# Where the block sums of y are split, and the order of ACT's bank copies, in an attention, mixture-of-experts and feed-forward kernel

## Chip, cores and metric

The kernel runs on one core of one Trainium2 chip. Times are microseconds (us) of device time for one execution; the time of a version is the median of its runs. The engines are TensorE (PE; its weight loads are listed apart as PEld), VectorE (DVE), ScalarE (ACT), GpSimd (Pool) and SyncE (SP), which issues nearly all DMAs, in order.

## What is computed

Three parts in a row on 2304 tokens of 512 values, all in float32.

```python
# 1. linear attention, 4 x 8 heads, 576 tokens, head size 64
kv = einsum('bhsd,bhse->bhde', k, v); out = einsum('bhsd,bhde->bhse', q, kv)
x = out / sqrt(mean(out * out) + 1e-6) * g_norm          # then to (2304, 512)
# 2. mixture of experts: 8 experts, 512 -> 1024 -> 512, one expert per token
expert_idx = argmax(x @ w_gate)
y = gate_w * (relu(x_e @ w1[e]) @ w2[e])                 # tokens beyond the capacity give 0
# 3. feed-forward: 512 -> 2048 -> 512
h = y @ w_in
out = where(h > 0, h, exp(min(h, 0)) - 1) @ w_out        # ELU
```

## The kernel before

Every float32 matrix product is made of three products of a faster type: a tile `t` is split into a high part `th` (an ACT copy that rounds, `split_hi`) and a low part `tl = t - th` (a subtraction on DVE or Pool, `split_lo`), and PE multiplies high by high, low by high and high by low (`three`, L636). So each operand that PE gets costs ACT one copy and DVE or Pool one subtraction.

**Expert steps.** The tokens are sorted by expert, and the experts run in order of falling load, each in NF = 8 steps, 64 in all (`step(u)`, L917). A step issues the weights of step u + 3 on SP (`expert_load`, two tiles of 256 KB), multiplies the tokens by 128 columns of w1 (`expert_h(u)`: 12 matmuls, then `hh` on ACT and `hl` on DVE from the bank `ph`), multiplies the hidden values of the step before by w2 (`expert_y(u - 1)`: 12 matmuls) and splits the weights of step u + 2 (`expert_split`). Some steps also convert a weight of the feed-forward part (`next(parts)`) or split the next expert's tokens (`window`). The order on every engine is the written one (`manual_schedule`). In the middle, after step 36, stands a branch that all engines take together.

**Block sums.** Three of the four quarters of the feed-forward part (by hidden columns) are computed in pairs of token blocks by Strassen's way (seven products instead of eight); its right operands are differences of blocks of y. The 2304 tokens are NB = 6 blocks of BT = 384, in three pairs m; for each pair and each of KH = 2 column groups k there are four differences, 24 in all. `right_sums` (L876) is a generator that makes one a call: it first finishes the one before (low part on DVE, then two DMAs of 192 KB on SP to `y_dram`), then subtracts on DVE into `tr`, and copies the high part into `th` on ACT. `th` and `tl` share the tag "e", two buffers for the two of them; `tr` has two buffers of tag "g". The first 16 sums (pairs 0 and 1) are called at the end of the expert steps listed in `SUMS` (37, 38, 40, 44, 45, 46, 48, 52, 53, 54, 56, 60, 61, 62, 63, 64) and the last finish in step 1 of the second layer; the eight of pair 2 (`late_sums`) in steps 1 to 9 of that layer, in spare halves of the output tile `part`.

**Second layer, first quarter.** `ffn_step(s)`, 24 steps (six blocks, four chunks of 128 hidden columns each): 12 matmuls of 384 columns, ELU (two ACT activations, `e`, and one DVE operation, `g`), its split `gh`, `gl` in the next step, and 9 matmuls of 512 columns two steps later into three accumulator banks of four; after a block's last chunk ACT copies the banks to `part` (L1029). In each block's second step the next block of y is split (`y_block_into`): four ACT copies, four Pool subtractions, DMAs. Two banks hold `ph`. One piece of weight preparation a step (`next(parts2)`) issues a load two pieces ahead.

**Second layer, the other quarters.** `pair_step(w, s)` (L1124), nine windows w of a pair and a quarter, two steps each. A step makes seven products of 6 matmuls, P1, P5, P2, P6, P3, P7, P4 in that order. P1, P6, P7, P4 accumulate on top of each other in the bank `pa`, P5 and P3 in `pd`, P2 in `pe`, and ACT copies the bank out between them (`s1`, `s5`, `u2`, `u3`), so that the next product into `pa` waits for the copy. Four blocks come out (c11, c12, c22, c21), each goes through `elu` and `elu_split`. In the gaps between products stand weight preparation (`gap`) and the units that multiply by w_out, whose sums DVE adds to `part`; at the end Pool scatters `part` to the output. The first six windows have the written order, the last three the order of the compiler's scheduler.

The lines that the change is about, of the sums:

```python
for ... in sums of a piece:            # right_sums, L890
    if last:
        finish()                       # split_lo (DVE) and 2 DMAs of the sum before
    r, t = tiles()
    nc.vector.tensor_tensor(out=r, in0=x, in1=y, op=ALU.subtract)
    split_hi(t, r)                     # ACT
    last.append((m, o, k, r, t))
    yield
```

Of the kernel before, what the change touches and what calls it, by code (L numbers as in the profile page):

```python
# [20 lines left out]
P = 128  # L21
# [20 lines left out]
def block_kernel(ctx, tc, qT, k, v, g_norm, w_gate, w1, w2, w_in, w_out, out, cap, **_):  # L42
# [13 lines left out]
    NB = 6  # L56
# [463 lines left out]
    def split_hi(dst, src):  # L520
        return nc.scalar.activation(dst[0], src, AF.Copy)  # L521

    def split_lo(dst, src, engine):
        return engine.tensor_tensor(out=dst[1], in0=src, in1=dst[0].bitcast(F32), op=ALU.subtract)  # L524
# [348 lines left out]
            for h, t in enumerate((yh, yl)):  # L873
                nc.sync.dma_start(out=y_dram[n // 2, o][:, h], in_=t[:, k:k + KH].bitcast(F32))

    def right_sums(pieces, tiles):  # L876


        last = []

        def finish():
            m, o, k, r, t = last.pop()
            split_lo(t, r, nc.vector)
            for h in range(2):
                nc.sync.dma_start(out=y_dram[m, o][:, h, k], in_=t[h].bitcast(F32))

        for m, k in pieces:
            b = [[yT[:, h * KH + k, (2 * m + n) * BT:(2 * m + n + 1) * BT] for n in range(2)] for h in range(2)]
            r = None
            for o, x, y in ((5, b[1][1], b[0][1]), (3, b[0][1], b[0][0]), (4, b[1][1], None), (6, b[1][0], None)):  # L890
                if last:
                    finish()
                y = r if y is None else y
                r, t = tiles()
                nc.vector.tensor_tensor(out=r, in0=x, in1=y, op=ALU.subtract)
                split_hi(t, r)
                last.append((m, o, k, r, t))
                yield
        finish()
        yield  # L900

    def small_tiles():
        t = [hp.tile([P, BT], F32R, name=n, tag="e", bufs=2) for n in ("th", "tl")]
        return hp.tile([P, BT], F32, name="tr", tag="g", bufs=2), t


    assert 3 * (N // E) >= 2 * BT and 6 * (N // E) >= 4 * BT
    early_sums = right_sums([(m, k) for m in range(2) for k in range(KH)], small_tiles)
    SUMS = [u for u in range(4 * NF + 5, NU) if u % NF in (0, 4, 5, 6)]
    SUMS = SUMS[:8] + [u for u in SUMS[8:] if u > 6 * NF] + [NU - 1, NU]  # L910

    APART = 4 * NF + 4
    FIRST = NF + 1
# [3 lines left out]
    def step(u):  # L917
        r, fc = divmod(u, NF)
        if u == 4:
            nc.gpsimd.memset(xT[:, :, N:NS], 0.0)  # L920
        more = r + 1 < E and placed["t"] < need[r + 1]
        expert_load(u + 3)
        if u == FIRST - 1:
            prep_load(2)
# [19 lines left out]
        if u == APART:  # L944
            place(NT, 0)
            beyond_windows()
        if u in SUMS:
            next(early_sums, None)
        if u == NU - 2 and cap >= BT:
            y_block_into(0)  # L950

# [79 lines left out]


    spare = part[:, NT // 2:].rearrange("p i c -> p (i c)")
    turn = {"n": 0}

    def spare_tiles():
        n = turn["n"] = 1 - turn["n"]
        at = [spare[:, (3 * n + i) * BT:(3 * n + i + 1) * BT] for i in range(3)]
        return at[0], (at[1].bitcast(F32R), at[2].bitcast(F32R))

    late_sums = right_sums([(NB // 2 - 1, k) for k in range(KH)], spare_tiles)
    NM = NB // 2
    steps = [(n, c) for n in range(NB) for c in range(NC2)]

# [72 lines left out]
    QUOTAS = ((6, 4), (6, 4), (6, 6))  # L1117
    pend = {}

    def finish_last():  # L1120
        if pend:
            elu_split(*pend.pop("x"))

    def pair_step(w, s):  # L1124
        between = {n: [] for n in range(3)}
        if s == 0 and w:
# [27 lines left out]
        pa = ps_h.tile([P, C], F32, name="pa", tag="ph")  # L1154
        pd = ps_x.tile([P, C], F32, name="pd", tag="pt")
        product(w, s, "P1", pa, True)
        s1 = wt.tile([P, BT], F32, name="s1")
        A.activation(s1, pa[:, :BT], AF.Copy)
        product(w, s, "P5", pd, True)
        s5 = wt.tile([P, BT], F32, name="s5", bufs=1)  # L1160
        A.activation(s5, pd[:, :BT], AF.Copy)
        pe = ps_x.tile([P, C], F32, name="pe", tag="pt")
        product(w, s, "P2", pe, True)
        finish_last()
        V.tensor_tensor(out=s1, in0=s1, in1=pe[:, :BT], op=ALU.add)
        g11 = elu(s1)
        gap(0)
        product(w, s, "P6", pa, False)
        u2 = hp.tile([P, BT], F32, name="u", tag="g", bufs=2)
        A.activation(u2, pa[:, :BT], AF.Copy)  # L1170
        elu_split(w, s, 0, 0, g11)
        product(w, s, "P3", pd, False)
        V.tensor_tensor(out=u2, in0=u2, in1=pd[:, :BT], op=ALU.add)
        g12 = elu(u2)
        gap(1)
        product(w, s, "P7", pa, False)
        u3 = hp.tile([P, BT], F32, name="u", tag="g", bufs=2)
        A.activation(u3, pa[:, :BT], AF.Copy)  # L1178
        elu_split(w, s, 1, 0, g12)
        V.tensor_tensor(out=s5, in0=s5, in1=u3, op=ALU.add)  # L1180
        g22 = elu(s5)
        gap(2)
        product(w, s, "P4", pa, False)
        elu_split(w, s, 1, 1, g22)
        pend["x"] = (w, s, 0, 1, elu(pa[:, :BT]))
        gap(3)

    def ffn_step(s):
        if 1 <= s <= len(steps):
            ffn_g(*steps[s - 1])  # L1190
        if s < len(steps):
            n, c = steps[s]
            ffn_h(n, c)
            if c == 1 and n + 1 < NB:
                y_block_into(n + 1)
        if 2 <= s < len(steps):
            ffn_out(*steps[s - 2])
        if s:
            next(early_sums, None)
            next(late_sums, None)  # L1200
            next(parts2)
        if s >= len(steps) - 4:
            for o in ((0, 3), (1, 4), (2, 5), (6,))[s - len(steps) + 4]:
                right_load(0, o)
# [9 lines left out]
    for w in range(by_hand, NW):  # L1214
        for s in range(2):
            pair_step(w, s)
    finish_last()

    w = NW - 1
    for b, t, ss in ((0, 2, (0,)), (1, 0, (0, 1)), (0, 0, (1,)), (0, 1, (1,)), (0, 2, (1,)), (1, 1, (0, 1)), (1, 2, (0, 1))):  # L1220
# [33 lines left out]
```

## Time and profile before

| | |
|---|---|
| median of 3 runs | 726.09 us (724.1 to 730.0) |
| the profiled execution's own time | 724.72 us |
| its span, first to last instruction | 722.9 us |
| mean granted TensorE clock | 0.990 |
| busy: PE, PEld, DVE, ACT, Pool | 683.1, 628.6, 497.6, 390.1, 105.0 us |
| DMA | 145.89 MB, 202 GB/s over the span |

The span is what the trace covers; 1.8 us of the execution lie around it. Busy shares are means over stages that have different limits, so the rows are read stage by stage: attention to 75 us, expert steps to 313 us (sums from 222), the join to 331, the second layer's first quarter to 423, the product steps to 705, the last units and the scatter to the end. PE's matmuls overlap and their ends are modelled; the distance from one start to the next says what one costs. A granted clock of 1.00 is 2.4 GHz, 0.50 is 1.2 GHz.

### The profile page before, as it was taken

The numbers are of one execution on the slowest core, as the hardware profiler recorded it, in microseconds if no ns is written. First come the engines' busy times: TensorE is split into PE (matmuls) and PEld (weight loads), VectorE is DVE, ScalarE is ACT, GpSimd is POOL, SyncE is SP. The second block draws the span as 40 slices with busy tenths as digits, with TensorE's granted clock in tenths as the row PEclk, the third lists the DMA queues.
The fourth block names the chain that finished last, engine by engine and source line by source line (L and its number), as shares of the span: only waits on it lengthen the run. The fifth ranks groups of instructions, "written<-read, shape, count | busy, mean of one in ns | idle before, by whom it ended". The sixth has DMA issues, their size and how long they took to land.

```text
span 722.9 us, 11978 instructions
## 1 busy us (share of the span) xinstructions
PE 683.1 (94%) x4236; PEld 628.6 (87%) x4236; DVE 497.6 (69%) x952; ACT 390.1 (54%) x818; POOL 105.0 (15%) x116
## 2 busy tenths in 40 slices
PE   8988999999989898969999998999999999999996
PEld 7888899999989887958789887988789898998895
DVE  4488768677776687747776646777687778955542
ACT  1463565555554564635665656664666555754550
POOL 7123851000000000022222200000000000002113
PEclk9998999999999999999999999999999999999999
DMA  8996956654555666744543627393637548165512
GB/s 281 395 310 166 295 175 197 185 176 147 187 164 177 216 199 220 218 175 149 197 173 116 260 119 290 134 342 120 264 113 311 230 163 321 59 261 219 205 57 88
DMA packets 67108, 145.89 MB, mean 202 GB/s; under 512 B 9312, under 2 KB 29280, under 8 KB 67040
## 3 DMA queue, kind: packets, MB, share of 16 engines
q1 hardware_dynamic: 63424, 135.44, 54.3%
q0 software_dynamic: 2880, 9.59, 3.8%
q8 instruction: 36, 0.59, 0.3%
q14 instruction: 32, 0.26, 0.1%
q10 hardware_dynamic: 736, 0.02, 0.1%
HBM read 118.92 MB, written 26.10 MB: 201 GB/s over the span
## 4 chain that ended last, share of the span: by engine, by line
PE 32%; issue 12%; DVE 10%; ACT 7%; DMA 3%; POOL 3%; SPq 0%; POOLq 0%; ACTq 0%; DVEq 0%
PE pa L1064 5%; PE acc L1105 3%; PE acc L1106 3%; PE acc L1104 3%; DMA y_dram<-th 3%; PE pd L1064 3%; PE ph L638 2%; PE ph L640 2%; POOL out L1112 2%; PE ph L639 2%; PE acc L1024 2%; PE acc L1025 2%; PE acc L1026 2%; PE pe L1064 1%; ACT e L1081 1%
## 5 line engine op out<-in xcount | busy, mean ns | idle before, releaser
L1064 PE MATMUL pa<-right,ab 128*128 128x384 f32 x432 | 86.1, 339 | 3.5 <-ACT u L1178 1.7
L1064 PEld LDWEIGHTS pa<-right,ab 128*128 128x128 f32 x432 | 76.7, 188 | 10.6 <-ACT u L1178 3.0
L638 PE MATMUL acc<-hh,w2h 128*128 128x288 f32 (+6 forms) x256 | 78.4, 306 | 7.7 <-ACT hh L657 7.7
L638 PE MATMUL ph<-xh,w1h 128*128 128x288 f32 (+6 forms) x256 | 78.2, 305 | 3.4 <-PEq L829 2.4
L640 PE MATMUL acc<-hl,w2h 128*128 128x288 f32 (+6 forms) x256 | 78.0, 305 | 0.0
L640 PE MATMUL ph<-xl,w1h 128*128 128x288 f32 (+6 forms) x256 | 77.7, 303 | 0.3 <-DVE xl L619 0.3
L639 PE MATMUL ph<-xh,w1l 128*128 128x288 f32 (+6 forms) x256 | 77.5, 303 | 0.0
L639 PE MATMUL acc<-hh,w2l 128*128 128x288 f32 (+6 forms) x256 | 77.0, 301 | 0.0
L1106 PE MATMUL acc<-w2h,gx 128*128 128x512 f32 x180 | 70.9, 394 | 0.0
L1105 PE MATMUL acc<-w2l,gx 128*128 128x512 f32 x180 | 70.7, 393 | 0.0
L1104 PE MATMUL acc<-w2h,gx 128*128 128x512 f32 x180 | 70.0, 389 | 0.0
L524 POOL TENSOR_TENSOR yl<-yT,yh 128x384 fp32r<-128x384 f32 x24 | 29.3, 1255 | 260.0 <-ACT yh L521 260.0
L658 DVE SCALAR_TENSOR_TENSOR hl<-ph,hh 128x288 fp32r<-128x288 f32 (+6 forms) x64 | 30.1, 470 | 49.8 <-ACT hh L657 49.7
L1112 POOL DMA_INDIRECT out<-part,ids x18 | 18.5, 1026 | 296.6 <-DVE part L1109 296.6
L657 ACT ACTIVATE hh<-ph 128x288 fp32r<-128x288 f32 (+6 forms) x64 | 26.7, 418 | 55.9 <-PE ph L640 55.5
L638 PEld LDWEIGHTS acc<-hh,w2h 128*128 128x128 f32 x256 | 48.5, 189 | 9.5 <-ACT hh L657 9.5
L524 DVE TENSOR_TENSOR w2l<-a,w2h 128x512 fp32r<-128x512 f32 x64 | 50.5, 789 | 7.9 <-ACT w2h L521 7.9
L638 PEld LDWEIGHTS ph<-xh,w1h 128*128 128x128 f32 x256 | 48.6, 190 | 3.8 <-ACTq L829 2.6
L640 PEld LDWEIGHTS acc<-hl,w2h 128*128 128x128 f32 x256 | 48.3, 188 | 1.6 <-DVE hl L658 1.5
L640 PEld LDWEIGHTS ph<-xl,w1h 128*128 128x128 f32 x256 | 48.6, 190 | 0.6 <-DVE xl L619 0.6
L639 PEld LDWEIGHTS ph<-xh,w1l 128*128 128x128 f32 x256 | 48.6, 190 | 0.0
L639 PEld LDWEIGHTS acc<-hh,w2l 128*128 128x128 f32 x256 | 48.4, 189 | 0.0
(219 smaller groups left out, 1647.8 us busy)
## 6 DMA issues: line engine op xcount, KB each, us to landing
right<-y_dram SPq DMA_DIRECT2D x63, 768.0 KB, 6.4
a<-w SPq DMA_DIRECT2D x128, 256.0 KB, 3.3
w<-w_in SPq DMA_DIRECT2D x16, 512.0 KB, 4.3
w<-w_out SPq DMA_DIRECT2D x16, 512.0 KB, 5.8
kt<-k SPq DMA_DIRECT2D x18, 256.0 KB, 6.6
vt<-v SPq DMA_DIRECT2D x18, 256.0 KB, 6.1
x_dram<-oz_all SPq DMA_DIRECT2D x18, 256.0 KB, 5.5
y_dram<-yh SPq DMA_DIRECT2D x9, 384.0 KB, 2.3
```

The source lines that it names most:

```text
L524: return engine.tensor_tensor(out=dst[1], in0=src, in1=dst[0].bitcast(F32), op=ALU.subtract)
L638: nc.tensor.matmul(out, lhsT=ah, rhs=bh, start=start, stop=False)
L639: nc.tensor.matmul(out, lhsT=al, rhs=bh, start=False, stop=False)
L640: nc.tensor.matmul(out, lhsT=ah, rhs=bl, start=False, stop=stop)
L657: nc.scalar.activation(hh[:, :W], ph[:, :W], AF.Relu)
L658: nc.vector.scalar_tensor_tensor(out=hl[:, :W], in0=ph[:, :W], scalar=0.0, in1=hh[:, :W].bitcast(F32), op0=ALU.max, op1=ALU.subtract)
L1024: nc.tensor.matmul(acc, lhsT=gh[:, ts], rhs=w2h, start=(c == 0), stop=False)
L1064: nc.tensor.matmul(ps[:, :BT], lhsT=x[:, cs], rhs=b[:, y, k], start=(start and k == 0 and n == 0), stop=(k == KH - 1 and n == 2), skip_gro ...
L1104: nc.tensor.matmul(acc, lhsT=gh[:, ts], rhs=w2h, start=(s == 0 and c == 0), stop=False)
L1105: nc.tensor.matmul(acc, lhsT=gh[:, ts], rhs=w2l, start=False, stop=False)
L1106: nc.tensor.matmul(acc, lhsT=gl[:, ts], rhs=w2h, start=False, stop=(s == 1 and c == 1))
L1112: put = nc.gpsimd.indirect_dma_start(out=out, out_offset=bass.IndirectOffsetOnAxis(ap=ids[:, i:i + 1], axis=0), in_=part[:, i], in_offset= ...
```

## The change

Three things. `right_sums` now allocates the split tiles, copies the high part and takes the low part in the call after the one that subtracts; both subtractions are on an engine that the caller names, DVE for the first 16 sums and Pool for the last eight. The first 17 calls are at the head of the expert steps in a new list, ahead of the step's weight loads and matmuls, the last of them at step 60, and none is left in the second layer. And in `pair_step` ELUs and splits move: each bank copy now comes ahead of the ELU of the block before, the ELU of c21 and the splits of c22 and c21 come in the next step, behind its copies of P1 and P5 and the product P2; `s5` has two buffers and `s1` one, where it was the other way round.

```diff
--- before.py
+++ after.py
@@ -873,14 +873,16 @@
             for h, t in enumerate((yh, yl)):
                 nc.sync.dma_start(out=y_dram[n // 2, o][:, h], in_=t[:, k:k + KH].bitcast(F32))
 
-    def right_sums(pieces, tiles):
+    def right_sums(pieces, raw_tile, split_tiles, engine):
 
 
         last = []
 
         def finish():
-            m, o, k, r, t = last.pop()
-            split_lo(t, r, nc.vector)
+            m, o, k, r = last.pop()
+            t = split_tiles()
+            split_hi(t, r)
+            split_lo(t, r, engine)
             for h in range(2):
                 nc.sync.dma_start(out=y_dram[m, o][:, h, k], in_=t[h].bitcast(F32))
 
@@ -891,23 +893,24 @@
                 if last:
                     finish()
                 y = r if y is None else y
-                r, t = tiles()
-                nc.vector.tensor_tensor(out=r, in0=x, in1=y, op=ALU.subtract)
-                split_hi(t, r)
-                last.append((m, o, k, r, t))
+                r = raw_tile()
+                engine.tensor_tensor(out=r, in0=x, in1=y, op=ALU.subtract)
+                last.append((m, o, k, r))
                 yield
         finish()
         yield
 
-    def small_tiles():
-        t = [hp.tile([P, BT], F32R, name=n, tag="e", bufs=2) for n in ("th", "tl")]
-        return hp.tile([P, BT], F32, name="tr", tag="g", bufs=2), t
+    def raw_small():
+        return hp.tile([P, BT], F32, name="tr", tag="g", bufs=2)
+
+    def split_small():
+        return [hp.tile([P, BT], F32R, name=n, tag="e", bufs=2) for n in ("th", "tl")]
 
 
     assert 3 * (N // E) >= 2 * BT and 6 * (N // E) >= 4 * BT
-    early_sums = right_sums([(m, k) for m in range(2) for k in range(KH)], small_tiles)
-    SUMS = [u for u in range(4 * NF + 5, NU) if u % NF in (0, 4, 5, 6)]
-    SUMS = SUMS[:8] + [u for u in SUMS[8:] if u > 6 * NF] + [NU - 1, NU]
+    early_sums = right_sums([(m, k) for m in range(2) for k in range(KH)], raw_small, split_small, nc.vector)
+    SUMS = (37, 38, 40, 41, 43, 44, 45, 46, 49, 51, 52, 53, 54, 56, 57, 58, 60)
+    assert SUMS[0] > 3 * NF and SUMS[8] > 6 * NF
 
     APART = 4 * NF + 4
     FIRST = NF + 1
@@ -919,6 +922,8 @@
         if u == 4:
             nc.gpsimd.memset(xT[:, :, N:NS], 0.0)
         more = r + 1 < E and placed["t"] < need[r + 1]
+        if u in SUMS:
+            next(early_sums)
         expert_load(u + 3)
         if u == FIRST - 1:
             prep_load(2)
@@ -944,8 +949,6 @@
         if u == APART:
             place(NT, 0)
             beyond_windows()
-        if u in SUMS:
-            next(early_sums, None)
         if u == NU - 2 and cap >= BT:
             y_block_into(0)
 
@@ -1031,14 +1034,20 @@
 
 
     spare = part[:, NT // 2:].rearrange("p i c -> p (i c)")
-    turn = {"n": 0}
-
-    def spare_tiles():
-        n = turn["n"] = 1 - turn["n"]
-        at = [spare[:, (3 * n + i) * BT:(3 * n + i + 1) * BT] for i in range(3)]
-        return at[0], (at[1].bitcast(F32R), at[2].bitcast(F32R))
-
-    late_sums = right_sums([(NB // 2 - 1, k) for k in range(KH)], spare_tiles)
+    turn = {"r": 0, "s": 0}
+
+    def spare_part(n):
+        return spare[:, n * BT:(n + 1) * BT]
+
+    def raw_spare():
+        turn["r"] += 1
+        return spare_part(turn["r"] % 2)
+
+    def split_spare():
+        turn["s"] += 1
+        return [spare_part(2 + 2 * (turn["s"] % 2) + h).bitcast(F32R) for h in range(2)]
+
+    late_sums = right_sums([(NB // 2 - 1, k) for k in range(KH)], raw_spare, split_spare, nc.gpsimd)
     NM = NB // 2
     steps = [(n, c) for n in range(NB) for c in range(NC2)]
 
@@ -1116,10 +1125,6 @@
 
     QUOTAS = ((6, 4), (6, 4), (6, 6))
     pend = {}
-
-    def finish_last():
-        if pend:
-            elu_split(*pend.pop("x"))
 
     def pair_step(w, s):
         between = {n: [] for n in range(3)}
@@ -1154,35 +1159,39 @@
         pa = ps_h.tile([P, C], F32, name="pa", tag="ph")
         pd = ps_x.tile([P, C], F32, name="pd", tag="pt")
         product(w, s, "P1", pa, True)
-        s1 = wt.tile([P, BT], F32, name="s1")
+        s1 = wt.tile([P, BT], F32, name="s1", bufs=1)
         A.activation(s1, pa[:, :BT], AF.Copy)
+        if pend:
+            g21 = elu(pend["c21"])
         product(w, s, "P5", pd, True)
-        s5 = wt.tile([P, BT], F32, name="s5", bufs=1)
+        s5 = wt.tile([P, BT], F32, name="s5")
         A.activation(s5, pd[:, :BT], AF.Copy)
+        if pend:
+            elu_split(*pend["g22"])
         pe = ps_x.tile([P, C], F32, name="pe", tag="pt")
         product(w, s, "P2", pe, True)
-        finish_last()
+        if pend:
+            elu_split(*pend["at"], g21)
         V.tensor_tensor(out=s1, in0=s1, in1=pe[:, :BT], op=ALU.add)
-        g11 = elu(s1)
         gap(0)
         product(w, s, "P6", pa, False)
         u2 = hp.tile([P, BT], F32, name="u", tag="g", bufs=2)
         A.activation(u2, pa[:, :BT], AF.Copy)
-        elu_split(w, s, 0, 0, g11)
+        g11 = elu(s1)
         product(w, s, "P3", pd, False)
         V.tensor_tensor(out=u2, in0=u2, in1=pd[:, :BT], op=ALU.add)
-        g12 = elu(u2)
         gap(1)
         product(w, s, "P7", pa, False)
         u3 = hp.tile([P, BT], F32, name="u", tag="g", bufs=2)
         A.activation(u3, pa[:, :BT], AF.Copy)
-        elu_split(w, s, 1, 0, g12)
         V.tensor_tensor(out=s5, in0=s5, in1=u3, op=ALU.add)
-        g22 = elu(s5)
+        elu_split(w, s, 0, 0, g11)
+        g12 = elu(u2)
         gap(2)
         product(w, s, "P4", pa, False)
-        elu_split(w, s, 1, 1, g22)
-        pend["x"] = (w, s, 0, 1, elu(pa[:, :BT]))
+        elu_split(w, s, 1, 0, g12)
+        g22 = elu(s5)
+        pend.update(c21=pa[:, :BT], g22=(w, s, 1, 1, g22), at=(w, s, 0, 1))
         gap(3)
 
     def ffn_step(s):
@@ -1196,7 +1205,6 @@
         if 2 <= s < len(steps):
             ffn_out(*steps[s - 2])
         if s:
-            next(early_sums, None)
             next(late_sums, None)
             next(parts2)
         if s >= len(steps) - 4:
@@ -1214,7 +1222,8 @@
     for w in range(by_hand, NW):
         for s in range(2):
             pair_step(w, s)
-    finish_last()
+    elu_split(*pend["g22"])
+    elu_split(*pend["at"], elu(pend["c21"]))
 
     w = NW - 1
     for b, t, ss in ((0, 2, (0,)), (1, 0, (0, 1)), (0, 0, (1,)), (0, 1, (1,)), (0, 2, (1,)), (1, 1, (0, 1)), (1, 2, (0, 1))):
```

## Rows read from the trace of the kernel before

**Rows 1.** page, part 1 (busy us, share of the span, xinstructions)
```profile
PE 683.1 (94%) x4236; PEld 628.6 (87%) x4236; DVE 497.6 (69%) x952; ACT 390.1 (54%) x818; POOL 105.0 (15%) x116
```

**Rows 2.** windows: length; PE, PEld, DVE, ACT, POOL busy; PEclk; DMA share; GB/s
```profile
222.00:313.00 91.00, 82.70 (x622) 79.15 (x620) 68.50 (x131) 49.94 (x106) 0.00 (x0) 1.00 0.63 201
313.00:325.60 12.60, 6.72 (x36) 5.44 (x36) 4.64 (x8) 4.21 (x12) 4.55 (x4) 1.00 0.48 189
326.00:329.40 3.40, 3.40 (x13) 3.40 (x12) 2.84 (x4) 2.67 (x7) 1.86 (x2) 0.53 0.00 0
331.00:370.00 39.00, 35.52 (x173) 30.49 (x172) 29.15 (x49) 23.97 (x53) 9.81 (x10) 1.00 0.52 182
420.00:520.00 100.00, 95.65 (x474) 84.33 (x473) 70.43 (x145) 58.20 (x128) 0.00 (x0) 1.00 0.57 211
520.00:705.00 185.00, 184.97 (x921) 166.08 (x920) 127.38 (x255) 107.33 (x230) 12.73 (x12) 1.00 0.50 189
```

**Rows 3.** waits, 222 to 313 us (total us, times, longest us)
```profile
ACT th L521 <- DMA y_dram<-th: 17.4, 6, 5.4
ACT th L521 <- DVE tr L895: 15.4, 8, 3.1
...
PE acc L638 <- ACT hh L657: 7.7, 8, 2.6
```

**Rows 4.** timeline of ACT, 231 to 239 us (start us, us, instruction)
```profile
237.70 0.52 ACT L521 ACTIVATE th<-tr 128x384 fp32r<-128x384 f32 x1 [5.41 <-DMA y_dram<-th]
```

**Rows 5.** timeline of PE, 258 to 261 us
```profile
258.49 0.29 PE L640 MATMUL ph<-xl,w1h 128*128 128x272 f32 x1
259.52 0.40 PE L638 MATMUL acc<-hh,w2h 128*128 128x288 f32 x1 [0.74 <-ACT hh L657]
...
260.25 0.29 PE L638 MATMUL acc<-hh,w2h 128*128 128x288 f32 x1
```

**Rows 6.** timeline of SP's queue, 253 to 255 us
```profile
253.73 0.33 SPq L885 DMA_DIRECT2D y_dram<-tl  x1
...
254.80 0.34 SPq L584 DMA_DIRECT2D a<-w  x1
```

**Rows 7.** tile a, 222 to 313 us: the DMAs' landing
```profile
DMA to landing us min/median/max: 2.6/3.8/6.3
```

**Rows 8.** timeline, 319 to 326 us
```profile
320.73 0.53 ACT L521 ACTIVATE th<-tr 128x384 fp32r<-128x384 f32 x1 [6.13 <-DMA y_dram<-th]
...
325.61 0.44 PE L638 MATMUL ph<-yh,w1h 128*128 128x384 f32 x1 [4.62 <-DVE g L1005]
```

**Rows 9.** timeline of DVE, 327 to 338 us
```profile
328.88 1.35 DVE L895 TENSOR_TENSOR part<-yT 128x384 f32<-128x384 f32 x1
...
337.30 0.55 DVE L895 TENSOR_TENSOR part<-yT 128x384 f32<-128x384 f32 x1
```

**Rows 10.** tile yl, whole span (duration in ns)
```profile
L524 POOL TENSOR_TENSOR yl<-yT,yh x24: 1000/1326/1502, 313.2 to 402.4; 128x384 fp32r<-128x384 f32 x24
```

**Rows 11.** waits, 331 to 420 us
```profile
ACT part L521 <- DVE part L895: 7.8, 5, 1.6
...
PE acc L1024 <- ACT part L1029: 2.2, 2, 1.3
...
PE ph L638 <- DVE g L1005: 1.2, 1, 1.2
```

**Rows 12.** waits, 420 to 565 us
```profile
PE pa L1064 <- ACT u L1178: 1.7, 3, 0.7
PE pa L1064 <- ACT u L1170: 1.5, 2, 1.1
```

**Rows 13.** timeline of PE, 443 to 446 us
```profile
443.83 0.39 PE L1105 MATMUL acc<-w2l,gx 128*128 128x512 f32 x1
444.06 0.40 PE L1106 MATMUL acc<-w2h,gx 128*128 128x512 f32 x1
445.59 0.62 PE L1064 MATMUL pa<-right,ab 128*128 128x384 f32 x2 [1.14 <-ACT u L1170]
```

## Prediction

> **What bounds the kernel now.** I began with the page's first part: TensorE (PE) is busy 94% of the span [rows 1], so the time is PE's work plus the places where PE stands. The second view is the table of windows [rows 2], read as a window's length minus PE's busy time. It says where that is: 91.0 - 82.70 = 8.3 us in the expert steps with block sums (222 to 313 us); 12.6 - 6.72 = 5.9 us at the join of the two layers (313 to 325.6), and then, right after PE's long stand, 3.4 us at a granted clock of 0.53, the 1.2 GHz level; 39.0 - 35.52 = 3.5 us early in the second layer (331 to 370); 100.0 - 95.65 = 4.4 us in the first product steps (420 to 520). From 520 to 705 PE stands nowhere (184.97 of 185.0 us), so whatever the change does there can only lose. The attention part isn't touched.
>
> The third view is who waited for whom, by stage. In the expert steps [rows 3] ACT waits 17.4 us for an earlier `th` to land in DRAM and 15.4 us for DVE's difference `tr`, both in front of a sum's high-part copy; PE waits for ACT's `hh`, 7.7 us at 8 stops. The timeline shows one [rows 4]: 5.41 us in front of the copy at 237.70, since `th` has a single buffer whose transfer was issued in the same call; the next `hh` stands behind that copy in ACT's queue. A stop costs more than its row's idle time [rows 5]: from the start at 258.49 to that at 260.25 lie four matmuls and 1.76 us, where four take 4 x 82.70/622 = 0.53 [rows 2]; so 1.23 us for 0.74 shown, 0.5 on top.
>
> **The early sums (DVE).** The edit moves `th`'s copy from behind its own difference to the head of a later step. Nothing is added: 16 copies, 16 differences, 16 low parts, 32 DMAs as before. Both causes go: the difference is a step old, and the earlier transfer was issued a step before. Ceiling: 7.7 + 8 x 0.5 = 11.7 us.
>
> What is late next? First DVE: 68.5 us of work [rows 2] plus five sum operations that ran after 313 (5 x 0.55 [rows 9] = 2.8) in 91 - 11.7 = 79.3 us, 90%. Second a ring through SP, whose queue is in order: a step's two sum DMAs now stand ahead of `expert_load(u + 3)`. From the low part's DMA to that of the second weight tile is 1.1 us [rows 6], the landing takes 3.8 us, 2.6 to 6.3 [rows 7]; the weight's split, a conversion and the next `th` are 0.52 each (the activation of [rows 4] as the estimate), the low part 0.55. That closes the ring two steps later: 1.1 + 3.8 + 3 x 0.52 + 0.55 = 7.0 us, where PE takes 48 x 0.133 = 6.4. So a sum that follows one in the step before may cost 0.3 us, and 10 of 16 do: 3 us; nothing at a 2.6 us landing, 16 us at 6.3 (9.5 - 6.4 = 3.1, halved, times 10). I take the median landing and a microsecond for DVE, 4 us left, and count 7.7 us.
>
> **The join.** The list of steps now ends at 60, so no sum runs in the last expert steps or the first one of the second layer. Now the `th` copy at 320.73 waits 6.13 us for a transfer, the last `yT` copies and the first ELU queue behind it on ACT, and PE stops 4.62 us [rows 8]; the clock loss follows. ACT's copy of the first y block, for which PE makes a short stop around 313, stands behind a `th` copy too. Idle 5.9 + 0.6 us (8.3 less the 7.7 of the experts), and 3.4 us at half rate = 1.7: I count 8.2 us, and set the restarts there, not priced by a row, against what stays. All of it stays if PE still stands long enough at the join to lose the clock; the y block's copies now start before PE needs them.
>
> **The late sums (Pool).** 8 differences and 8 low parts, 0.55 us each on DVE, go to Pool, which takes 1.33 us at the median (1.00 to 1.50) for the same subtraction [rows 10]: 16 x 1.33 = 21 us on an engine that has only blocks of four here. ACT then has no wait for DVE's difference (7.8 us at five places), which puts it behind PE, so that the bank copies `part` come late, 2.2 us at two stops [rows 11]. With the 1.2 us that the last early sum's transfer costs it is the 3.5 us idle; with 0.16 a stop (below) 4.0.
>
> New waits: after a y block Pool owes four low parts ahead of the sum, some 5 us; at the next step's `th` ACT waits for Pool, and a conversion and the next ELU queue behind. Two banks let PE run a step ahead, 21 x 35.52/173 = 4.3 us [rows 2], so that is mostly covered. Steps 1 to 9 hold 12 + 16 = 28 Pool operations x 1.33 = 37 us, and nine steps are 39: no reserve. SP holds two DMAs behind the low part and the next weight load behind those; it is two pieces ahead, so nothing. Between the 4.0 and a loss of 3 (rival B) I count 3.2 us, near the first, since the second asks that every operation be the slowest.
>
> A row speaks against this move: beside a Pool subtraction the same DVE difference takes 1.35 us, without it 0.55 [rows 9]. The Trainium skill, in SBUF — State Buffer (section "SBUF: two separate sides"), goes further: DVE and Pool share a pair of ports under an exclusive lock that is held for the whole instruction, so a DVE operation with two SBUF inputs and a Pool operation shut each other out. By that rule in full 21 us of DVE would stand, against 39.0 - 29.15 = 9.9 us free in the window 331 to 370 and 16 x 0.55 = 8.8 us that leave it; the 2.6 us over would take back most of this part, and the profiled time would be some 703. The trace bears it out in part: the lengthening is 0.8 us, less than a whole Pool operation, and I go by the 0.8.
>
> **The product steps.** The same instructions in another order: ACT copies a bank as soon as its product ends, an ELU follows one product later, and the ELUs and splits of the last two blocks move past the next step's first copies. Now PE waits 1.7 us (3 stops) for `u` L1178 and 1.5 us (2) for `u` L1170 [rows 12], the rest of the 4.4 us at smaller stops. A start at 445.59 where 444.29 was due (0.23 after 444.06) is 1.30 us for 1.14 shown [rows 13], 0.16 on top; 5 x 0.16 makes 5.2 us. The `u` of that stop stands behind an ELU of two activations, about 1.04 us, nearly all of the 1.14. Conversions and output copies stay ahead of some copies, so I leave 0.8 us and count 4.4. Who waits for the later ELUs: DVE's `s1` now waits for the copy behind P6, and DVE's additions queue behind that (rival C). The unit that takes the last block's low part stands behind three products and another unit. `s5` takes the second buffer that `s1` gives up: no new wait. The end keeps its order: 0. The last three of nine windows aren't ordered by hand, and PE doesn't stand there: 0.
>
> **Sum.** 7.7 + 8.2 + 3.2 + 4.4 = 23.5 us. The profiled execution took 724.7 (span 722.9 and 1.8 around it), which gives 701.2; the median of the runs shown is 1.4 above it, so 702.6.
>
> **Rivals.** *A, the ring through SP binds.* For: 4.9 of its 7.0 us are in rows, and the same bytes in less time raise DMA's share of 0.63 [rows 2]. Against: steps without a sum give time back. At a 5 us landing (ring 8.2, 10 x 0.9 = 9 us left) the experts gain 2.7 instead of 7.7: 707.6; at 6.3 they lose 4: 714.
>
> *B, Pool bounds the second layer's first steps.* At 1.50 us, 28 x 1.5 = 42 us in 39: 3 us lost and 3.2 not won, 708.8. Full port lock is this case too.
>
> *C, slower: the product steps.* DVE waits, in order, for an exp that now stands behind the copy of P6. If that adds 2 us to each of 18 steps of 15.6 us (281/18), 36 us come on top and 4.4 aren't won: 743. It makes the kernel slower by over 1% from (19.1 + 7.3)/18 = 1.5 us a step on. Against: DVE is busy 70.43 of 100 us there [rows 2], 4.6 us free in each step.
>
> *D, the copies don't come first where it counts*, because conversions ahead of them are what PE waits for: the product steps give 0, 707.0.
>
> **Chances.** Forecast 0.57, with its own range of 696 to 708; A 0.17; B 0.07; D 0.11; C 0.05; 0.03 for stops that all come back elsewhere. The low end, 694, is every stop gone (11.7 + 8.2 + 4.0 + 5.2 = 29.1 us: 697) and 3 us of restarts that the rows don't price; the high end, 716, is A's far end and 2 us more. By over 1% (below 718.8; the runs of before lie 0.8% apart, so 1% is about what can be told from no change) faster are the first four, 0.92, less 0.04 for A and B together with a bad join: 0.88. Within 1%: 0.07. Slower: 0.05.
>
> **What would show it.** Right: `th` without idle time for `tr` and under 5 us for landings; no PE stop over 1 us between 222 and the second layer's tenth step, and no half clock at the join; differences on Pool at about 1.3 us; `pa` stops under 1 us in all. Wrong: PE stops for `hh` with ACT waiting for `a` or DVE late with `tl` (A), for `g` with ACT waiting for Pool (B), for units with DVE waiting for an exp (C), for `u` behind conversions (D).

## The result, and the profile after

The median is 706.59 us (four runs, 705.1 to 707.2) against 726.40 (four runs): a ratio of 0.972, 95% interval 0.9677 to 0.9763, so 19.8 us faster. In a second series, beside some of the experiments, the same kernel gave 0.9703 (0.9668 to 0.9739). The profiled execution took 707.2 us, its span is 705.4.

The first part of the page, which answers to [rows 1]:

```profile
PE 677.7 (96%) x4236; PEld 628.4 (89%) x4236; DVE 495.7 (70%) x936; ACT 389.7 (55%) x818; POOL 123.1 (17%) x132
```

The 16 subtractions of the late sums have gone from DVE to Pool (952 to 936, 116 to 132). PE has the same 4236 matmuls in 5.4 us less busy time, so it not only stands less, it also takes less time for the same work. Where, the windows tell. Their borders are instructions of PE: the first matmul behind the branch, the first on `yh`, and the first and last product into `pa`; 331 cuts the second layer behind the join. First the kernel before (length; PE, PEld, DVE, ACT, POOL busy; PEclk; DMA share; GB/s):

```profile
216.70:313.10 96.40, 87.99 (x648) 84.45 (x648) 70.20 (x133) 52.06 (x110) 0.00 (x0) 0.98 0.63 202
313.10:331.00 17.90, 12.11 (x56) 10.47 (x57) 9.09 (x13) 7.91 (x19) 8.01 (x7) 0.90 0.39 154
331.00:424.10 93.10, 89.62 (x445) 79.48 (x444) 63.29 (x108) 56.71 (x122) 21.34 (x18) 1.00 0.52 192
424.10:702.90 278.80, 274.42 (x1362) 244.96 (x1361) 195.09 (x393) 161.88 (x348) 12.73 (x12) 1.00 0.53 200
```

The same stages after:

```profile
220.66:316.50 95.84, 89.34 (x661) 85.97 (x662) 72.79 (x140) 56.59 (x117) 3.72 (x4) 0.98 0.68 223
316.50:331.00 14.50, 14.50 (x78) 13.44 (x78) 9.24 (x13) 8.06 (x18) 8.21 (x8) 1.00 0.43 156
331.00:413.70 82.70, 82.56 (x412) 73.80 (x411) 56.76 (x85) 53.60 (x115) 35.60 (x30) 1.00 0.53 200
413.70:685.40 271.70, 271.70 (x1362) 245.51 (x1361) 195.40 (x393) 159.70 (x348) 12.65 (x12) 1.00 0.54 205
```

Length minus PE's busy time is where PE stands: 8.4, 5.8, 3.5 and 4.4 us before; 6.5, 0, 0.1 and 0 after. The join has no stop and no half rate any more (PEclk 0.90 to 1.00), and the second layer runs without a stop to its end. The expert steps have kept most of theirs. Before, the first y matmuls ran among those of the last expert step: 648 matmuls lie in its first window, 661 after. These 13 are 13 x 0.133 = 1.7 us, which I put with the experts, here and in the table below. So the expert steps went from 98.1 to 95.8 us (-2.3), the second layer's first quarter from 109.3 to 97.2 (-12.1), the product steps from 278.8 to 271.7 (-7.1): 21.5 us. In the profiled execution 4.0 us are lost ahead of the branch, which PE leaves at 220.66 instead of 216.71: a stop of 4.3 us at 79 us, in the first matmuls of the expert part, where the kernel before stands 1.0 us, and PEclk 0.50 from 77 to 84 us. The change doesn't touch these matmuls. The second series' execution has neither, its branch at 216.06 and a span of 700.8.

What keeps the expert steps? Who waited for whom, 222 to 304 us, after (total us, times, longest), to be held against [rows 3]:

```profile
ACT w1h L521 <- DMA a<-w: 15.7, 11, 2.2
...
ACT th L521 <- DMA y_dram<-th: 6.2, 4, 3.2
...
PE acc L640 <- DVE hl L658: 4.9, 8, 1.3
...
ACT w2h L521 <- DMA a<-w: 2.9, 4, 1.4
...
PE acc L638 <- ACT hh L657: 1.3, 1, 1.3
```

ACT's wait for `tr` (15.4 us) is gone, that for `th`'s transfer down from 17.4 to 6.2. In their place ACT waits 18.6 us for weights `a` to land, and PE 4.9 us for DVE's `hl`. The chain of work that ended last, 244 to 260 us, shows the loop (start us, us, what):

```profile
244.91 0.48 DVE tl L524
...
245.41 0.33 SPq L887
...
246.53 0.34 SPq L584
...
247.44 5.75 DMA y_dram<-th
...
253.30 0.53 ACT th L521
...
253.86 0.32 DVE tl L524
...
255.17 0.52 DVE w1l L524
...
255.77 0.59 DVE w2l L524
256.37 0.72 DVE xl L634
257.09 0.48 DVE tl L524
257.58 0.33 SPq L887
...
258.66 5.29 DMA a<-w
```

A sum's DMA on SP's queue waits for DVE's low part; the weight loads (L583, L584) stand behind it, and behind those the next sum's high part, which takes 5.75 us to land; the high-part copy after it waits for that. Then its low part and, in DVE's order, low parts of weights and tokens come ahead of the next sum's low part, which holds up SP again, and weights land 5.29 us after their issue. None of these pieces is PE's. It is the ring of rival A, with the transfer of `th` as a second way round and DVE's queue as a part of both. The chain's other landings up to 304 us are

```profile
269.95 2.69 DMA a<-w
...
274.95 3.02 DMA y_dram<-th
...
278.62 3.54 DMA y_dram<-th
...
282.82 2.98 DMA y_dram<-th
...
288.12 3.64 DMA a<-w
...
297.41 3.34 DMA y_dram<-tl
...
302.49 3.01 DMA a<-w
```

and, ahead of the piece above, one of weights of 4.23 us at 238.70.

### The profile page after: what moved, and what is told of

Read it like the earlier page. It is cut to its first block, busy times and chain, and to the rows that moved or that the text cites. A ratio compares the mean times of both kernels' runs of the same rounds, so it can differ in the third digit from the quotient of the medians.

```text
span 705.4 us, 11922 instructions
## 1 busy us (share of the span) xinstructions
PE 677.7 (96%) x4236; PEld 628.4 (89%) x4236; DVE 495.7 (70%) x936; ACT 389.7 (55%) x818; POOL 123.1 (17%) x132
## 4 chain that ended last, share of the span: by engine, by line
PE 49%; DMA 6%; issue 5%; DVE 3%; POOL 2%; ACT 2%; SPq 1%; POOLq 0%; ACTq 0%; DVEq 0%
PE pa L1073 10%; PE acc L1114 6%; PE acc L1115 6%; PE acc L1113 6%; PE pd L1073 5%; DMA a<-w 3%; PE pe L1073 3%; DMA y_dram<-th 2%; PE acc L1029 2%; PE ph L638 2%; PE ph L640 2%; PE ph L639 2%; PE acc L1028 2%; PE acc L1027 2%; POOL yl L524 1%
## 5 line engine op out<-in xcount | busy, mean ns | idle before, releaser
L1121 POOL DMA_INDIRECT out<-part,ids x18 | 18.4, 1023 | 289.6 <-DVE part L1118 283.1
L524 POOL TENSOR_TENSOR yl<-yT,yh 128x384 fp32r<-128x384 f32 x24 | 27.8, 1187 | 223.7 <-DVE w2l L524 194.4
L524 DVE TENSOR_TENSOR w2l<-a,w2h 128x512 fp32r<-128x512 f32 x64 | 52.3, 817 | 10.3 <-ACT w2h L521 9.3
L521 ACT ACTIVATE w1h<-a 128x512 fp32r<-128x512 f32 x64 | 40.1, 627 | 20.6 <-DMA a<-w 20.6
```

The lines of the kernel that those rows point to most:

```text
L1121: put = nc.gpsimd.indirect_dma_start(out=out, out_offset=bass.IndirectOffsetOnAxis(ap=ids[:, i:i + 1], axis=0), in_=part[:, i], in_offset= ...
```

## Experiments

Ratios are to the kernel before on the same chip, with 95% intervals. The stage lengths are from each profiled execution, with the borders above.

| kernel | ratio | expert steps | PE idle there | 2nd layer, first quarter | product steps |
|---|---|---|---|---|---|
| before | 1 | 98.1 | 8.4 | 109.3 | 278.8 |
| after, second series (e0) | 0.9703 (0.9668 to 0.9739) | 95.8 | 5.4 | 97.2 | 271.7 |
| e1 sums only | 0.9841 (0.9816 to 0.9867) | 95.1 | 5.4 | 97.2 | 278.9 |
| e2 products only | 0.9900 (0.9874 to 0.9927) | 95.9 | 6.2 | 109.3 | 271.7 |
| e3 late sums on DVE | 0.9723 (0.9697 to 0.9748) | 97.2 | 6.8 | 96.8 | 271.7 |
| e4 loads first | 0.9618 (0.9592 to 0.9643) | 93.3 | 3.9 | 97.2 | 271.7 |
| e13 the same again | 0.9624 (0.9573 to 0.9674) | 90.4 | 4.9 | 97.2 | 271.7 |
| e5 early sums on Pool | 0.9763 (0.9727 to 0.9799) | 97.0 | 8.0 | 97.2 | 271.7 |
| e6 sums by Pool's queue | 0.9740 (0.9686 to 0.9795) | 92.5 | 3.9 | 97.1 | 271.8 |
| e8 old list | 0.9689 (0.9653 to 0.9725) | 86.9 | 1.1 | 105.0 | 271.7 |
| e10 spread list | 0.9691 (0.9650 to 0.9732) | 91.6 | 5.2 | 97.2 | 271.8 |
| e11 spread, loads first | 0.9572 (0.9532 to 0.9612) | 87.1 | 2.4 | 97.2 | 271.7 |
| e12 split at once | 0.9869 (0.9828 to 0.9909) | 108.3 | 15.1 | 97.2 | 271.7 |

The column of the expert steps is good to some 2 or 3 us: e2 has before's code there and lies 2.2 below it, and the stage holds stretches of half rate that differ from execution to execution (last section). The rows of e10 to e13, which ran together on another chip than e0 to e8, lack the half rate behind the branch (3.4 us of it, worth 1.7). The profiled execution of e4 is its slowest run, 701.7 us where the others took 694.5 to 697.1. Where a verdict hangs on less, the ratios decide.

**The two halves of the change (e1, e2).** e1 is the kernel after with the old `pair_step`; e2 is the kernel before with the new one, whose core is

```diff
         A.activation(s1, pa[:, :BT], AF.Copy)
+        if pend:
+            g21 = elu(pend["c21"])
...
         A.activation(u2, pa[:, :BT], AF.Copy)
-        elu_split(w, s, 0, 0, g11)
+        g11 = elu(s1)
```

> The changed sums (early on DVE, late on Pool, new list of steps) with the product steps in their old order. My theory now, from the two traces: the sums' part gives about 13 us at the join and early in the second layer and 2 us in the expert steps, the new product order about 7 us, so this kernel at 706.6 + 7 = 713 to 714 us, with PE stops for u in the product steps as before. Rival (the product order gives the 4.4 us that was forecast, or nothing, and the sums the rest): 711, or 707.

> The old sums with the new order of the product steps. Theory: 726.4 - 7 = 719 us, the product steps without PE stops, the join and the expert steps as before. Rival (the two parts depend on each other, because the old late sums leave ACT and DVE behind when the product steps begin): 722 to 726.

Measured: the sums alone give 11.3 us (711.30 against 722.58), the products alone 7.1 (715.48). Their shares, 1.6% and 1.0%, add up to 2.6% where the whole gives 2.8 and 3.0, a difference inside the intervals, and each half has the whole's lengths in its own stages: no interaction shows. With the old order e1 has the old stops, the rows of [rows 12] again (PE's waits, 400 to 550 us):

```profile
PE pa L1073 <- ACT u L1187: 1.7, 3, 0.7
PE pa L1073 <- ACT u L1179: 1.5, 2, 1.1
```

**Pool for the late sums (e3).**

```diff
-    late_sums = right_sums([...], raw_spare, split_spare, nc.gpsimd)
+    late_sums = right_sums([...], raw_spare, split_spare, nc.vector)
```

> All of the change, but the eight late sums subtract on DVE instead of Pool. Theory: what helped there is the split one call later, not the engine, and Pool's 21 us are hidden: same as the changed kernel within 1 us, 706 to 708, with DVE's forms beside Pool at 0.55 us more often. Rival 1 (Pool is what frees ACT): 710, with PE stops at the bank copies of the output. Rival 2 (the port lock costs): 704 to 705.

Measured: no difference in the time, 0.9723, nor in the stage, 96.8 against 97.2 us. So Pool gave nothing here. Nor is it the list: in e8, with the old one, PE stands nowhere from 331 to 408 us (77.20 us busy of 77.20). That leaves the later split, by which ACT no longer meets a difference made in the same step. The tile `part` after, 318 to 405 us (duration in ns, min/median/max):

```profile
L524 POOL TENSOR_TENSOR part<-part x8: 1012/1028/1521, 328.9 to 359.7; 128x384 fp32r<-128x384 f32 x8
L897 POOL TENSOR_TENSOR part<-yT x4: 1325/1330/1464, 326.9 to 347.0; 128x384 f32<-128x384 f32 x4
```

and with DVE (e3):

```profile
L524 DVE TENSOR_TENSOR part<-part x8: 546/548/1303, 326.5 to 355.8; 128x384 fp32r<-128x384 f32 x8
L897 DVE TENSOR_TENSOR part<-yT x4: 545/548/553, 320.8 to 343.4; 128x384 f32<-128x384 f32 x4
```

ACT does wait for Pool, more than it did for DVE before [rows 11] (waits after, 320 to 405 us):

```profile
ACT part L521 <- POOL part L897: 9.3, 6, 3.1
```

but PE stands 0.1 us in the whole stage: that wait is covered. In e3 ACT's wait for DVE's difference is 0.5 us.

**The order on SP's queue (e4, e13).** The step's weight loads go ahead of the sum's call.

```diff
+        expert_load(u + 3)
         if u in SUMS:
             next(early_sums)
-        expert_load(u + 3)
```

> All of the change, but the early sums are called right behind the step's weight loads instead of ahead of them, so the loads no longer queue behind a sum's two DMAs of the same step. Theory (the ring through SP costs what is left in the expert steps, about 9 us of PE stops between 222 and 304 us): ACT's 17 us of waits for a fall to under 6, and the time to 700 to 703. Rival 1 (DMA bandwidth, not order): 705 to 708, the waits for a the same size. Rival 2 (DVE is late because tl and tr stand ahead of hl): 705 to 708, the stops at hl stay at 4.9 us.

> The change with the calls behind the weight loads, run again beside the two spread lists on one chip: ratio 0.960 to 0.965 as before; above the one of the spread list with loads first by 0.003 or more if density has a cost of its own (the wait for th), the same as that within 0.002 if not.

Measured twice: 0.9618 and 0.9624, some 6 us faster than the change as it stands, which was run beside neither. e4's interval lies clear of both of the change's, and e13's of the first; its upper end, 0.9674, lies 0.0006 inside that of e0. ACT's waits for `a` are gone altogether; what is left, 222 to 304 us of e4:

```profile
ACT th L521 <- DMA y_dram<-th: 16.0, 8, 4.6
...
PE acc L638 <- ACT hh L657: 2.5, 1, 2.5
...
PE acc L640 <- DVE hl L658: 1.3, 3, 0.7
```

The `th` copy still waits for the landing before it, now for 16.0 us, but that loop no longer holds the weights, and of PE's waits 3.8 us stay where 6.4 were. The edit moves nothing but the order of issue on SP. So the ring through SP is real, and by the ratios it costs about 6 us.

**Is it DVE? (e5)** The early sums' subtractions on Pool, which is idle there: `nc.vector` becomes `nc.gpsimd` for `early_sums`.

> All of the change, but the early sums subtract on Pool, which has nothing else to do in those steps, so DVE has 32 operations less (some 15 us by starts) and no wait for th ahead of hl. If DVE's work or its waiting in order makes PE stop for hl (4.9 us in 222 to 304 us), those stops go and the ratio falls by 0.005 to 0.007. Theory (the ring through SP): the low part is slower on Pool (1.3 against 0.55 us), so the sum's DMAs and the weight loads behind them come later; ACT's waits for a grow from 17 us to over 20, and the ratio is 0.970 to 0.978, no better.

Measured 0.9763, not faster than the change. The waits, 222 to 304 us:

```profile
ACT w1h L521 <- DMA a<-w: 13.2, 10, 2.1
```

With 31 subtractions on Pool instead of DVE in this window ACT waits 15.1 us for weights, `w2h` included, against 18.4 in e0. They didn't grow to over 20, as had been expected, and they didn't shrink much. Taking that load off DVE doesn't help. What DVE's order costs in the loop this doesn't price, since the same subtractions take longer on Pool.

**Another queue for the sums (e6).** The early sums' DMAs are issued by Pool instead of SP:

```diff
-                nc.sync.dma_start(out=y_dram[m, o][:, h, k], in_=t[h].bitcast(F32))
+                (queue or nc.sync).dma_start(out=y_dram[m, o][:, h, k], in_=t[h].bitcast(F32))
```

> All of the change, but the early sums' DMAs are issued on Pool's queue: same bytes, same order of everything else, and SP's weight loads have no sum ahead of them. Theory (order in SP's queue, not bandwidth): ACT's waits for a under 5 us, ratio 0.960 to 0.965, as with the loads issued first. Rival (the same bytes have to pass in less time): waits for a over 12 us, ratio 0.970 to 0.975.

Measured 0.974 with runs from 701.6 to 708.3: the gain that was expected isn't there. Yet the profile shows what e4's does: no wait of ACT for `a`, expert steps of 92.5 us. The span doesn't have it, because the end is longer. The last step of the chain, e6:

```profile
692.81 1.19 POOLq L1259
```

and the change's second series:

```profile
695.55 1.19 POOLq L1259
```

From there to the end of the span are 700.9 - 692.8 = 8.1 us in e6 and 700.8 - 695.6 = 5.2; in every other profile of this record they are 5.2 or 5.3. What happens in these 2.8 us the trace doesn't show; it stays open.

**Places against split (e8, e12).** e8 keeps the later split but takes the old list, called at the end of the step, so behind the step's weight loads, and the last in the second layer's step 1; e12 keeps the new places, but copies the high part in the call that subtracts. Both keep the late sums of the kernel after. In e8

```diff
-    SUMS = (37, 38, 40, 41, 43, 44, 45, 46, 49, 51, 52, 53, 54, 56, 57, 58, 60)
+    SUMS = [u for u in range(4 * NF + 5, NU) if u % NF in (0, 4, 5, 6)]
+    SUMS = SUMS[:8] + [u for u in SUMS[8:] if u > 6 * NF] + [NU - 1, NU]
...
-        if u in SUMS:
-            next(early_sums)
         expert_load(u + 3)
...
+        if u in SUMS:
+            next(early_sums, None)
```

and in e12, for the early sums,

```diff
...
                 engine.tensor_tensor(out=r, in0=x, in1=y, op=ALU.subtract)
-                last.append((m, o, k, r))
+                t = split_tiles() if at_once else None
+                if at_once:
+                    split_hi(t, r)
+                last.append((m, o, k, r, t))
```

> All of the change, but the early sums are called where they were before: at the end of the old kernel's steps, the last of them in the second layer's step 1. Tells apart what splitting one call later gives from what the new places give. Theory: the join's gain (some 9 us) comes mostly from the places, since the old ones leave two sums and their landings in front of the first ELU: PE stops over 3 us at the join again, ratio 0.980 to 0.985. Rival (the split one call later alone does it, as the th of a call no longer waits for the DMA issued in that call): no stop over 1 us at the join, ratio 0.970 or below.

> All of the change, but the early sums' high part is copied right behind its difference again, in the same call: new places, old split. Theory: the split one call later is what the expert steps need, since ACT otherwise waits for tr and for the th whose DMA has just been issued, at the head of a step, ahead of hh; PE stops for hh over 15 us in 222 to 304 us, ratio 0.985 to 0.995. Rival (the new places alone do it): 0.970 to 0.975.

Measured: e8 is as fast as the change (0.9689), where 0.980 to 0.985 was expected, and e12 loses more than half of the gain (0.9869). By stages that makes a square. With the early sums split at once, expert steps and first quarter are 98.1 + 109.3 in the old places (before) and 108.3 + 97.2 in the new ones (e12); with the later split 86.9 + 105.0 (e8) and 95.8 + 97.2 (the change). The later split takes 11.2 us from the expert steps in the old places and 12.5 in the new. The new list, called ahead of the loads, takes 7.8 us from the first quarter and adds 8.9 to the expert steps: as the change has it, it moves the cost. But "places" are two things here, the steps of the list and the place within the step, and by the ratios of e4 and e13 some 6 us go with the second: behind the loads the same list has 93.3 and 90.4 us, a spread one 87.1 (e11, below), all three with the first quarter at 97.2. e8's windows, the expert steps and the join:

```profile
216.32:301.50 85.18, 84.08 (x648) 83.57 (x649) 70.37 (x133) 54.23 (x112) 1.52 (x2) 0.98 0.67 227
301.50:331.00 29.50, 23.50 (x115) 21.22 (x114) 17.97 (x26) 14.27 (x31) 14.95 (x14) 0.88 0.46 174
```

PE stands 1.1 us in the first and 6.0 in the second, and there the clock falls, as before. PE stops where it did in [rows 8], for `g`; here the ELU's own `e`, which shares `th`'s buffers, is what waits for the landing (waits of e8, 304 to 330 us):

```profile
ACT e L1005 <- DMA y_dram<-th: 6.8, 2, 4.9
...
PE ph L638 <- DVE g L1008: 5.5, 2, 5.1
```

In e12 the old waits are back in the expert steps, larger than in [rows 3] (222 to 304 us):

```profile
ACT th L521 <- DMA y_dram<-th: 21.8, 7, 4.7
...
ACT th L521 <- DVE tr L898: 17.8, 7, 4.2
PE acc L638 <- ACT hh L657: 8.9, 7, 3.4
```

**A thinner list (e10, e11).** The 17 calls spread to step 62; e11 has e4's order as well.

```diff
-    SUMS = (37, 38, 40, 41, 43, 44, 45, 46, 49, 51, 52, 53, 54, 56, 57, 58, 60)
+    SUMS = (38, 39, 41, 42, 44, 46, 47, 49, 50, 52, 54, 55, 57, 58, 60, 61, 62)
```

> All of the change with the 17 calls spread over steps 38 to 62, never three in a row while weights are still loaded. Theory (a sum that follows one in the step before costs, through SP and the single th): PE stops in 222 to 304 us fall from some 6 us of idle time to under 3, no stop at the join, ratio 0.962 to 0.967. Rival 1 (the last calls, at 60 to 62, put the stop at the join back): 0.970 or above. Rival 2 (density doesn't matter): 0.970 to 0.973.

> The spread list, and the calls behind the step's weight loads. If order in SP and density are one cause (the ring), the second remedy adds little to either: ratio 0.958 to 0.963. If they are two (weights late, and the single th), it adds up: 0.953 to 0.957.

Measured: the spread list alone is no faster than the change (0.9691), where 0.962 to 0.967 was expected; with the loads first it gives 0.9572, the fastest kernel of all, 697.0 us against 726.1. Whether it beats e13 (0.9624 beside it on the same chip) the intervals don't settle, 0.9532 to 0.9612 and 0.9573 to 0.9674. In e10 `th` hardly waits, and the weights wait as before (222 to 304 us):

```profile
ACT w1h L521 <- DMA a<-w: 20.2, 13, 2.4
...
ACT th L521 <- DMA y_dram<-th: 0.6, 1, 0.6
```

In e11 the weights' wait is small, that for `th` is 9.9 us where e4 had 16.0, and no stop comes back at the join, though its last call is at step 62:

```profile
ACT th L521 <- DMA y_dram<-th: 9.9, 7, 2.3
...
ACT w1h L521 <- DMA a<-w: 2.6, 2, 1.9
```

Density alone isn't the cause, then: of the two remedies only the place in SP's queue gains by itself.

**The reference (e0).** The kernel after once more, beside e5, e6 and e8.

> The changed kernel unaltered, beside the three below on one chip. Ratio to the kernel before 0.970 to 0.975. PE's 4.3 us stop at 79 us, which the first profile of it shows and none of four sister kernels does, is a matter of the single execution: not there (theory), or there again (rival: the change moves something ahead of the expert steps).

Measured 0.9703, in agreement with 0.972. The stop at 79 us isn't in its profile, but it is no matter of a single execution: e10 to e13, the four kernels of the other chip, all have one there, of 3.4 to 3.9 us. Why, and whether the kernel before has it on that chip, no profile shows.

## Why the prediction was right, and where it was not

A saving of 23.5 us was forecast; 19.8 (726.40 to 706.59) and 21.4 (724.04 to 702.67) were measured. That the second median is the 702.6 us of the forecast is luck, since its kernel before is 2 us faster than the one forecast from. And two terms of the sum were off, in opposite directions, 5.4 us too much and 2.7 too little, so that the sum is better than its parts.

**Early sums: 7.7 us forecast, 2.3 found.** The ceiling was right within the scatter: 11.7 us, and e8, where the later split works in the old places, takes 11.2. The term that was mis-sized is what stays of it, "4 us left"; it was 9.4. The ring through SP that the prediction drew is real, and e4 and e13 bear it out: the same work with the loads first gets some 6 us back. Its landing was not what was wrong. The five weight landings on the chain above are 4.23, 5.29, 2.69, 3.64 and 3.01 us, 3.8 in the mean, which is the prediction's figure; in e0, with the same 95.8 us, the median of all of them is 3.2. The step that failed is "Both causes go [...] the earlier transfer was issued a step before": the wait for the earlier `th` was put at nothing, and so the ring was closed with one landing in it. The chain passes through four landings of `th`, 15.3 us together, and one of `tl`; ACT still waits 6.2 us for `th`, 16.0 in e4. DVE got one microsecond; between two low parts of the chain above lie 2.9 us of its other work. And the sums that moved out of the second layer were counted as DVE time only, not as turns of the ring. How the 9.4 us divide among these the runs don't show: e10 has hardly a wait for `th` left, and PE stands 5.2 us where e0 has 5.4. Rival A came true in its mechanism. That its first price, a gain of 2.7 us, is close to the 2.3 found is luck, because it asked for landings of 5 us.

**The join: 8.2 us forecast.** 5.8 us of idle time and the half rate, 3.4 us of it worth 1.7, are gone. e8 shows that it is the list: with the old one the stop and the clock loss return, and the quarter is 7.8 us longer. What the prediction did not see is that the list, called ahead of the weight loads, pays for this gain with 8.9 us in the expert steps; called behind them it keeps the gain at less cost (e4, e13, e11).

**Late sums: 3.2 us forecast, 3.3 of idle time found** (3.5 to 0.1). The reason was half wrong: the title of that part was Pool, but e3 gives the engine no share. Pool's new waits came, 9.3 us on ACT at six places, the longest 3.1 us where some 5 had been drawn, and are hidden, so rival B did not come.

**Product steps: 4.4 us forecast, 7.1 found.** The mechanism was right: no stop is left in the stage, and e2 alone gives it. The term mis-sized is the restart, "5 x 0.16". PE's 4.38 us of idle time are gone, but the same 1362 matmuls also take 271.70 us busy instead of 274.42: 2.7 us over the nine waits that PE has there in the kernel before, 0.30 a stop in the mean. And of the 0.8 us left for conversions ahead of the copies nothing came. Rivals C and D are refuted: PE doesn't stand from 413.7 to 685.4 at all.

**The lock of the ports.** Beside Pool's subtractions DVE's take longer, as the row of before had shown, 1.37 us for one of 0.55. DVE's timeline after:

```profile
326.02 1.37 DVE L524 TENSOR_TENSOR gl<-g,gh 128x384 fp32r<-128x384 f32 x1
```

Over the second layer's first quarter DVE has 113 operations in e3 and 97 in the second series. First e3's window:

```profile
314.90:411.70 96.80, 96.56 (x489) 87.58 (x488) 63.99 (x113) 62.36 (x133) 23.20 (x21) 1.00 0.52 193
```

and that of the second series:

```profile
311.90:409.10 97.20, 97.06 (x489) 87.21 (x488) 66.02 (x97) 61.66 (x133) 43.85 (x37) 1.00 0.51 193
```

In e3 the 16 sums took 10.3 us (eight of 0.74 and eight of 0.55, some beside Pool's `yl`), so DVE would be busy 53.7 us without them, and in the second series its other work took some 12 us longer. Pool's 16 took 20.3 us there (eight of 1.20, eight of 1.33). The Trainium skill's page SBUF — State Buffer (section "SBUF: two separate sides") has a DVE operation with two SBUF inputs and a Pool operation that reads SBUF shut each other out for the whole instruction; by that, as an estimate, up to 20.3 us could have shown on DVE. The trace has some 60% of it, which doesn't test the rule, since it isn't counted how many of Pool's operations met such a one of DVE's. PE saw none of it. The prediction's "some 703" for the rule in full is 701.2 + 2.6 = 703.8 by its own terms.

## What to carry to other kernels

When a producer and the copy that reads it are put a step apart, look at what its DMAs then stand in front of on their queue: here the weight loads came behind them, and swapping two lines of issue order was worth some 6 us, about a third of the whole change. Walk every way round such a ring, the transfer out of a single buffer and the other work of an in-order engine included, before you price it with one landing. And test a new list of places separately from a new dependency, and the place within a step separately from the list: here the dependency removed stops in either list, while the list, called ahead of the loads, moved them.

## What the runs showed of the hardware

- A stop of PE in the product steps costs 0.30 us in the mean on top of the idle time that its rows show: the same 1362 matmuls were busy 274.42 us with nine such waits and 271.70 with none (e1, with the stops, has 274.55 for 1363).
- Half rate differs between profiles of the same code, which were not all taken on one chip. Behind the branch PE stands 2.0 to 2.5 us in every profile; ten of the fourteen then show PEclk 0.50 for about 3.4 us, and e10 to e13, the four of the other chip, show 1.00. These four and the first profile of the kernel after have PEclk 0.50 near 80 us, where PE had stopped 3.4 to 4.3 us; the other nine have neither. e4 shows 0.50 for 6.8 us from 293 us, behind a stop of 2.46 us, and e13, the same kernel on the other chip, nowhere in that stage: for their 660 matmuls e4's PE was busy 89.4 us, e13's 85.5.
- With the early sums' DMAs on Pool's queue the end of the program took 2.8 us more (e6: 8.1 us from its last queue instruction, 5.2 or 5.3 in all other profiles), some 390 us after the last of these DMAs.
- DVE's two-input subtraction of 128x384 takes 0.55 us, and 1.2 to 1.4 us beside a Pool subtraction, which itself takes 1.0 to 1.5 us.
